# A linear-attention and gated feed-forward kernel: batch 1 turned wholly by DMA, its q loaded first, batch 2's loads queued later

## Chip, cores, metric

One core of a Trainium2 chip. The metric is device microseconds (us) for one execution.

## The reference, cut to what matters

```python
B, H, S, D, KP = 8, 8, 1024, 64, 64           # q, k, v: [B, H, S, D] float32
k_proj = einsum('ks,bhsd->bhkd', E, k);  v_proj = einsum('ks,bhsd->bhkd', F, v)
attn = softmax(q @ k_proj.T / sqrt(D));  a = attn @ v_proj
x = a.transpose(0, 2, 1, 3).reshape(8192, 512)
g = x @ w_gate;  out = (g * sigmoid(g) * (x @ w_val)) @ w_out      # d_ff = 1536
```

## The kernel before

The feed-forward part is 16 tiles of 512 tokens (two per batch). For each of the 12 slices of `d_ff` TensorE does a gate group, a value group (4 matmuls of 128x512 each) and, of the tile before, one group of the output product. After each gate group, and again after each value group with its output group, there is a *slot*, in which pieces of the next batch's attention are put. Batches count from 0, so `b == 1` is the second batch.

q and the normalised scores must each be turned (transposed) before TensorE can use them. Two ways exist: on TensorE (`u_T`, `u_A`, with a copy out of PSUM) or by a DMA transpose from SyncE (`u_TD`, `u_AD`). `BY_DMA` lists the halves that go by DMA.

```python
BY_DMA = [(b, ch) for b in range(1, B) for ch in range(CH)][1:]      # all but (1, 0)

def u_TD(b, ch):                                    # q half by DMA
    t = aw.tile([P, 2 * H, P], BF16, name="qTd", tag="qTd")
    nc.sync.dma_start_transpose(out=t[:], in_=qb[b, ch][:].rearrange("p h j d -> p (h j d)"))
def u_AD(b, ch):                                    # normalised scores by DMA -> AT
    ...
# loads are issued by GpSimd in program order, among its normalisations (u_N)
load_wo(0); load_wo(1); load_k(1)
...
put(20, load_q, 1, 0); put(20, load_v, 1); put(20, load_q, 1, 1)
for b in range(2, B):
    s0 = 48 * (b - 1) - (12 if b == 2 else 24)
    put(s0, load_k, b); put(s0 + 2, load_v, b); put(s0 + 4, load_q, b, 0); put(s0 + 6, load_q, b, 1)
```

`u_KV` projects k and v (8 matmuls each, on `kb` and `vb`), `u_KT` turns the projected k, `u_S` computes scores, `u_R` and `u_N` normalise them, `u_PV` is the product with v (`pv`). SyncE also issues every output store, in one stream with the DMA transposes.

The softmax here doesn't subtract the row's maximum and nothing guards it: scores larger than these inputs give would overflow.

Of the kernel before, what the change touches and what calls it, by code (L numbers as in the profile page):

```python
# [15 lines left out]
B = 8  # L16
# [11 lines left out]
CH = 2  # L28
CW = 512
NIT = B * CH * NFT  # L30
BY_DMA = [(b, ch) for b in range(1, B) for ch in range(CH)][1:]


@with_exitstack
def kernel(
# [49 lines left out]
    def load_k(b, h0=0, h1=H):  # L85
        if h0 == 0:
            kb[b] = kv_pool.tile([P, H, NJ, D], BF16, name="kb", tag="kb")
        nc.gpsimd.dma_start(  # L88
            out=kb[b][:, h0:h1].rearrange("p h j d -> p h (j d)"),
            in_=k[b, h0:h1].rearrange("h (p j) d -> p h (j d)", j=NJ),  # L90
        )
# [10 lines left out]
    def load_q(b, ch, parts=1):  # L102
        t = q_pool.tile([P, H, 4, D], BF16, name="qb", tag="qb")
        qb[b, ch] = t
        n = H // parts
        for i in range(parts):
            nc.gpsimd.dma_start(  # L107
                out=t[:, i * n : (i + 1) * n].rearrange("p h j d -> p h (j d)"),
                in_=q[b, i * n : (i + 1) * n].rearrange("h (p c j) d -> p c h (j d)", c=2, j=4)[:, ch],
            )  # L110

    def load_w_gv(c0, c1, which=(0, 1)):
        cs = slice(c0 * P, c1 * P)
        for wsrc, wdst in [((moe_w_gate, wg), (moe_w_val, wv))[i] for i in which]:
            nc.gpsimd.dma_start(
                out=wdst[:, :, cs],
                in_=wsrc[:, cs].rearrange("(t p) c -> p t c", p=P),
            )

    def load_wo(i):  # L120
        nc.gpsimd.dma_start(
            out=wo[:, 6 * i : 6 * (i + 1), :],
            in_=moe_w_out[6 * i * P : 6 * (i + 1) * P, :].rearrange("(t p) c -> p t c", p=P),
        )
# [93 lines left out]
    def u_S(b, u, at="a"):  # L218
        ch, w = divmod(u, 4)
        g, i = divmod(w, 2)  # L220
        ps = bank(at, [P, 4, P], FP32, "sc")
        if (b, ch) in BY_DMA:
            t = qT[b, ch, "d"][:].rearrange("p (h i) t -> p i h t", i=2)[:, i, 4 * g : 4 * g + 4]
# [163 lines left out]
    def put(s, fn, *a):  # L387
        slots[s].append((fn, a))

    def place(b):  # L390
        s0 = 48 * (b - 1)
        if b == 1:
            put(30, u_TD, 1, 1)
            put(34, u_KV, 1, "k")
            put(36, u_KT, 1)
            put(40, u_KV, 1, "v")
            sa = (37, 38, 39, 40, 48, 50, 52, 54)
            tt = (35, 36, 37, 38)
            ta = (41, 42, 43, 44)
            put(57, u_AD, 1, 1)  # L400
            sp = (43, 44, 45, 46, 66, 67, 68, 69)
        else:
            put(s0, u_KV, b)
            put(s0 + 3, u_KT, b)
            o = 14 if b == 2 else 6
            put(s0 + (3 if b == 2 else -6), u_TD, b, 0)
            put(s0 + (5 if b == 2 else -4), u_TD, b, 1)
            sa = [s0 + o + 3 * j for j in range(NJ)]
            put(sa[3] + 4, u_AD, b, 0)
            put(sa[7] + 4, u_AD, b, 1)  # L410
            sp = [s0 + i for i in (39, 41, 43, 45, 57, 59, 61, 63)]
        for j in range(NJ):
            if (b, j // 4) not in BY_DMA:
                put(tt[j], u_T, b, j)
                put(ta[j], u_A, b, j)
            put(sa[j], u_S, b, j)
            put(sa[j] + 1, u_R, b, j)
            put(sa[j] + 1, u_N, b, j)
        for i in range(8):
            put(sp[i], u_PV, b, i // 4, i % 4)  # L420
# [5 lines left out]
    with tc.manual_schedule():  # L426
        load_k(0, 0, 4)
        ef = []
        for which, src in (("E", E), ("F", F)):
            raw = const.tile([KP, S], FP32, name=f"{which}raw")  # L430
            nc.sync.dma_start(out=raw[:], in_=src)
            ef.append(raw)
        zeros = const.tile([P, CW], BF16, name="zeros")
        nc.vector.memset(zeros[:], 0.0)
        make_identity(nc, ident_fp[:])
        make_identity(nc, ident_bf[:])
        for i in range(2):
            nc.vector.memset(BD[i][:], 0.0)
            nc.vector.memset(BDV[i][:], 0.0)

        def turn(which):
            for half in range(2):
                ps = bank("v", [P, 4, KP], FP32, "efp")
                for i in range(4):
                    j = 4 * half + i
                    nc.tensor.transpose(
                        out=ps[:, i, :],
                        in_=ef[which][:, bass.ds(j, P, step=NJ)],
                        identity=ident_fp[:KP, :KP],
                    )  # L450
                js = slice(4 * half, 4 * half + 4)
                copy((nc.scalar, nc.vector)[which], (ET, FT)[which][:, js, :], ps[:])

        def warm(n):

            ps = bank("v", [P, CW], FP32, "warm")
            for _ in range(n):
                nc.tensor.matmul(
                    out=ps[:], lhsT=zeros[:, 0:P], rhs=zeros[:],
                    start=True, stop=True,  # L460
                )


        load_k(0, 4, 8)
        load_q(0, 0, 2)
        load_v(0, (0, 4, 8))
        load_w_gv(0, 1)
        load_w_gv(1, 2)
        load_w_gv(2, 4)
        warm(8)  # L470
        turn(0)
        turn(1)
        warm(7)
        u_KV(0, "k", (0, 4), at="y")
        warm(2)
        u_KT(0, at="v", prs=(0, 2))
        warm(2)
        u_KV(0, "k", (4, 8), at="y")
        warm(2)
        u_KT(0, at="v", prs=(2, 4))  # L480
        u_T(0, 0, "a", nc.scalar)
        u_T(0, 1, "a", nc.vector)
        u_T(0, 2, "a", nc.scalar)
        u_S(0, 0, "g")
        u_T(0, 3, "v", nc.vector)
        u_S(0, 2, "g")
        u_S(0, 1, "a")
        u_S(0, 3, "a")
        u_R(0, 0)
        u_N(0, 0)  # L490
        u_R(0, 2)
        u_N(0, 2)
        load_w_gv(4, 6, (0,))
        u_KV(0, "v", (0, 4), at="y")
        warm(1)
        u_A(0, 0, nc.scalar)
        u_R(0, 1)
        u_N(0, 1)
        u_R(0, 3)
        u_N(0, 3)  # L500
        u_A(0, 2, nc.scalar)
        u_KV(0, "v", (4, 8), at="y")
        load_w_gv(4, 6, (1,))
        load_q(0, 1)
        load_w_gv(6, 8)
        load_w_gv(8, 10)
        load_w_gv(10, 12)
        load_wo(0)
        load_wo(1)
        load_k(1)  # L510
        warm(1)
        u_PV2(0, 0, 0, 0, nc.scalar)
        u_PV2(0, 0, 1, 0, nc.vector)
        u_A(0, 1, nc.scalar)
        u_A(0, 3, nc.vector)
        f_mm(0, 0, 0, 0)
        f_mm(0, 0, 1, 0)
        u_PV2(0, 0, 0, 1, nc.scalar)
        u_PV2(0, 0, 1, 1, nc.vector)
        f_mm(0, 1, 0, 0)  # L520
        f_mm(0, 1, 1, 0)

        for i, u in enumerate(range(4, 8)):
            put(12 + i, u_T, 0, u)
            put(14 + i, u_S, 0, u)
            put(15 + i, u_R, 0, u)
            put(15 + i, u_N, 0, u)
            put(19 + i, u_A, 0, u, nc.scalar)
        put(21, u_PV, 0, 1, 0)
        put(22, u_PV, 0, 1, 1)  # L530
        put(23, u_PV, 0, 1, 2)
        put(23, u_PV, 0, 1, 3)
        put(20, load_q, 1, 0)
        put(20, load_v, 1)
        put(20, load_q, 1, 1)
        for b in range(1, B):
            place(b)
        for b in range(2, B):
            s0 = 48 * (b - 1) - (12 if b == 2 else 24)
            put(s0, load_k, b)  # L540
            put(s0 + 2, load_v, b)
            put(s0 + 4, load_q, b, 0)
            put(s0 + 6, load_q, b, 1)

        for s in slots:
            slots[s].sort(key=lambda x: x[0] not in (load_k, load_v, load_q))


        ypart = defaultdict(list)
        for c in range(B * CH - 1):  # L550
            for n in range(NFT):
                f = n if c else 4 + (2 * n + 1) // 3
                ypart[(c + 1) * NFT + f].append((c, n))

        for t in range(NIT):
            c, f = divmod(t, NFT)
            i = 1 if t < 2 else None
            f_g(c, f, i)
            run_slot(2 * t)
            f_v(c, f, i)  # L560
            for a in ypart.pop(t, ()):
                f_y(*a)
            run_slot(2 * t + 1)
        for n in range(9):
            f_y(B * CH - 1, n)
        f_y_last(B * CH - 1, 3)
        assert not slots and not ypart
# [29 lines left out]
```

## Time and profile before

| | before |
|---|---|
| time, median (lowest to highest) | 573.88 us (572.83 to 574.1, 3 runs) |
| TensorE busy, granted clock | 561.2 of 572.4 us, 1.000 |
| k, v of batch 2 issued / landed | 47.9, 48.7 / 67.5, 74.1 us |
| projection of batch 2 starts | 88.2 us |

The waits of TensorE in the kernel before (what waited, on what: us in total, times, longest). All lie in the first 22 us; none is a wait in mid-kernel.

```profile
PE kvp L147 <- DMA kb<-in_k_dram: 1.3, 2, 1.0
PE warm L458 <- DVE zeros L434: 1.2, 1, 1.2
PE kvp L147 <- DMA vb<-in_v_dram: 1.0, 2, 0.6
PE qTp L193 <- DMA qb<-in_q_dram: 0.4, 1, 0.4
```

### The profile page before, as it was taken

The page shows a single profiled execution, that of the slowest core. Times are in us where ns is not written, and L with a number is a line of the kernel's source. Part 1 is how long each engine was busy: PE and PEld are TensorE (multiplying, and loading weights), DVE is VectorE, ACT ScalarE, POOL GpSimd, SP SyncE. Part 2 cuts the span into 40 slices and gives each one's busy share as a digit, 9 for nine tenths or more (in the row PEclk, how much of TensorE's full clock was granted, in tenths as well). Part 3 has the DMA queues.
Part 4 walks back from the last instruction along what each step waited for, and adds up shares of the span by engine and source line. Part 5 has one row for each costly group of instructions (what it writes and reads, how often), then busy time and mean ns, then how long its engine had stood idle before and what let it go on. Part 6 is the DMA issues. An engine that isn't in the chain of part 4 may idle for free.

```text
span 572.4 us, 7867 instructions
## 1 busy us (share of the span) xinstructions
PE 561.2 (98%) x2910; PEld 268.6 (47%) x2967; DVE 336.8 (59%) x580; ACT 237.0 (41%) x416; POOL 107.9 (19%) x121
## 2 busy tenths in 40 slices
PE   8899999999999999999999999999999999999997
PEld 4654544444444444444444444444444444444444
DVE  2787566666466744766556665567546674554550
ACT  1655444353425434444335434354342543443232
POOL 6734131234002400124001330023200220000000
PEclk9999999999999999999999999999999999999999
DMA  9999993539901698037951399204990124100012
GB/s 160 196 200 206 201 161 74 93 64 196 201 37 41 110 190 157 18 75 129 187 108 38 59 179 195 63 22 88 197 176 37 42 52 74 38 37 25 31 39 92
DMA packets 105927, 61.34 MB, mean 107 GB/s; under 512 B 58016, under 2 KB 97696, under 8 KB 105888
## 3 DMA queue, kind: packets, MB, share of 16 engines
q0 software_dynamic: 42288, 29.89, 36.1%
q1 hardware_dynamic: 63312, 30.68, 25.1%
q8 instruction: 23, 0.38, 0.3%
q10 hardware_dynamic: 288, 0.26, 0.1%
q14 instruction: 16, 0.13, 0.1%
HBM read 60.29 MB, written 16.78 MB: 135 GB/s over the span
## 4 chain that ended last, share of the span: by engine, by line
PE 94%; DMA 2%; POOL 1%; ACT 1%; issue 1%; DVE 0%; POOLq 0%
PE yps L360 29%; PE vps L322 29%; PE gps L322 29%; PE kvp L147 3%; PE sc L227 2%; DMA vb<-in_v_dram 2%; PE pv L285 2%; PE aTp L274 0%; ACT xT L135 0%; PE qTp L193 0%; POOL kb L88 0%; PE kTp L172 0%; POOL qb L107 0%; ACT th L334 0%; PE pv L300 0%
## 5 line engine op out<-in xcount | busy, mean ns | idle before, releaser
L341 DVE SCALAR_TENSOR_TENSOR s<-th,gps 128x512 f32<-128x512 f32 x192 | 130.5, 680 | 138.0 <-ACT th L334 137.8
L322 PE MATMUL gps<-xT,wg 128*128 128x512 bf16 (+1 forms) x755 | 195.7, 377 | 1.2
L322 PE MATMUL vps<-xT,wv 128*128 128x512 bf16 (+1 forms) x761 | 195.9, 377 | 0.8
L360 PE MATMUL yps<-wo,hT 128*128 128x512 bf16 (+2 forms) x761 | 191.5, 376 | 0.8
L334 ACT ACTIVATE th<-gps 128x512 f32<-128x512 f32 x192 | 114.6, 597 | 162.6 <-PE gps L322 155.1
L346 DVE TENSOR_TENSOR hT<-s,vps 128x512 bf16<-128x512 f32 x192 | 132.0, 688 | 22.1 <-PE vps L322 1.5
L360 PEld LDWEIGHTS <-hT 128*128 128x128 bf16 x780 | 76.2, 98 | 89.9
L258 POOL TENSOR_TENSOR AAd<-ee,rr 128x512 bf16<-128x512 f32 x52 | 54.1, 1040 | 319.5 <-issue 168.4
L322 PEld LDWEIGHTS <-wv 128*128 128x128 bf16 x776 | 73.9, 98 | 82.9 <-issue 3.3
L322 PEld LDWEIGHTS <-wg 128*128 128x128 bf16 x776 | 74.0, 98 | 81.3 <-issue 0.6
L370 ACT ACTIVATE ysb<-yps 128x512 f32<-128x512 f32 (+1 forms) x65 | 38.4, 590 | 78.1 <-PE yps L360 74.4
L135 ACT CAST xT<-pv 128x512 bf16<-128x512 f32 x62 | 36.1, 585 | 51.3 <-PE pv L285 50.3
L242 DVE TENSOR_REDUCE zz<-ee 128x8 f32<-128x512 f32 x64 | 43.5, 679 | 17.9 <-ACT ee L231 17.9
L231 ACT ACTIVATE ee<-sc 128x512 f32<-128x512 f32 x64 | 37.9, 595 | 17.4 <-PE sc L227 17.4
L285 PE MATMUL pv<-AT,BDV 128*128 128x512 bf16 x60 | 22.6, 379 | 0.1
L227 PEld LDWEIGHTS <-qTd 128*128 128x128 bf16 x208 | 16.0, 98 | 12.3
L227 PE MATMUL sc<-BD,qTd 128*128 128x128 bf16 x208 | 20.1, 219 | 0.1
L135 DVE CAST BDV<-kvp 64x256 bf16<-64x256 f32 x14 | 6.0, 426 | 22.1 <-ACT ks L157 19.1
L258 POOL TENSOR_TENSOR AA<-ee,rr 128x512 bf16<-128x512 f32 x10 | 10.3, 1038 | 35.2 <-DVE rr L244 33.6
L147 PE MATMUL kvp<-kb,ET 128*64 128x512 bf16 (+1 forms) x72 | 15.5, 357 | 1.3 <-DMA kb<-in_k_dram 1.3
L244 DVE RECIPROCAL rr<-zz 128x8 f32<-128x8 f32 x64 | 13.0, 203 | 6.2
L147 PE MATMUL kvp<-vb,FT 128*64 128x512 bf16 (+1 forms) x72 | 15.5, 358 | 1.0 <-DMA vb<-in_v_dram 1.0
(49 smaller groups left out, 144.8 us busy)
## 6 DMA issues: line engine op xcount, KB each, us to landing
out_dram<-ysb SPq DMA_DIRECT2D x63, 256.0 KB, 2.3
qb<-in_q_dram POOLq DMA_DIRECT2D x15, 512.0 KB, 16.6
kb<-in_k_dram POOLq DMA_DIRECT2D x7, 1024.0 KB, 11.6
vb<-in_v_dram POOLq DMA_DIRECT2D x7, 1024.0 KB, 14.2
wo<-in_moe_w_out_dram POOLq DMA_DIRECT2D x2, 768.0 KB, 14.8
wg<-in_moe_w_gate_dram POOLq DMA_DIRECT2D x5, 256.0 KB, 10.4
wv<-in_moe_w_val_dram POOLq DMA_DIRECT2D x5, 256.0 KB, 10.4
kb<-in_k_dram POOLq DMA_DIRECT2D x2, 512.0 KB, 8.7
```

What stands on the lines that cost most here:

```text
L135: (nc.scalar.copy if eng is nc.scalar else eng.tensor_copy)(out=out, in_=in_)
L147: nc.tensor.matmul(out=t[lo : lo + 64, h0:h1].rearrange("p h d -> p (h d)"), lhsT=w[:, j, :], rhs=src[b][:, h0:h1, j, :], start=(j == 0), ...
L227: nc.tensor.matmul(out=ps[:, n, :], lhsT=t[:, n, :], rhs=BD[b % 2][:, 4 * g + n, :], start=True, stop=True)
L231: nc.scalar.activation(out=e[:].rearrange("p h j k -> p (h j k)"), in_=ps[:].rearrange("p a k -> p (a k)"), func=AF.Exp, scale=scale,)
L242: nc.vector.reduce_sum(out=z[:], in_=e[:], axis=AX.X)
L258: eng.tensor_tensor(out=a.rearrange("p j h k -> p h j k"), in0=ee.pop((b, u))[:], in1=rr.pop((b, u))[:].unsqueeze(3).to_broadcast([P, 4, 2 ...
L322: nc.tensor.matmul(out=ps[:, ts], lhsT=(wg, wv)[w][:, kt, f * P : (f + 1) * P], rhs=x[:, kt, ts], start=(kt == 0), stop=(kt == NKT - 1),)
L334: nc.scalar.activation(out=th[:], in_=ps[:], func=AF.Tanh, scale=0.5)
L341: nc.vector.scalar_tensor_tensor(out=s1[:], in0=th[:], scalar=1.0, in1=g[:], op0=ALU.add, op1=ALU.mult)
L346: nc.vector.tensor_tensor(out=hT[c][:, f, :], in0=s1[:], in1=ps[:], op=ALU.mult)
L360: nc.tensor.matmul(out=yy[c][:, cs], lhsT=hT[c][:, f, i * P : (i + 1) * P], rhs=wo[:, f, cs], start=(f == 0), stop=(f == NFT - 1),)
L370: nc.scalar.activation(out=ysb[:, cs], in_=yy[c][:, cs], func=AF.Copy, scale=0.5)
```

## The change

Intent: take the last transposes after batch 0 off TensorE, by turning batch 1's first half by DMA as well. To have its q in time, that half is loaded ahead of k and the output weights. To keep batch 1's DMA transposes free of other traffic, batch 2's loads are put at slots 50 to 52, and batch 2's projection, scores and transposes move back.

```diff
-BY_DMA = [(b, ch) for b in range(1, B) for ch in range(CH)][1:]
+BY_DMA = [(b, ch) for b in range(1, B) for ch in range(CH)]
@@ place(b), b == 1 (u_T, u_A of the first half removed)
-            put(34, u_KV, 1, "k"); put(36, u_KT, 1)
+            put(22, u_TD, 1, 0)
+            put(29, u_KV, 1, "k"); put(32, u_KT, 1)
-            sa = (37, 38, 39, 40, 48, 50, 52, 54)
+            sa = (35, 36, 37, 38, 48, 49, 50, 51)
+            put(41, u_AD, 1, 0); put(45, u_TD, 1, 1)
@@ place(b), b >= 2 (only b == 2 changes)
-            put(s0, u_KV, b); put(s0 + 3, u_KT, b)
-            o = 14 if b == 2 else 6                     # scores start at s0 + o
+            put(s0 + (12 if b == 2 else 0), u_KV, b)
+            put(s0 + (15 if b == 2 else 3), u_KT, b)
+            o = 17 if b == 2 else 6
@@ order of loads
+        load_q(1, 0)
+        load_k(1)
         load_wo(0)
         load_wo(1)
-        load_k(1)
-            s0 = 48 * (b - 1) - (12 if b == 2 else 24)
+            s0 = 48 * (b - 1) - 24
+            at = (50, 50, 51, 52) if b == 2 else (s0, s0 + 2, s0 + 4, s0 + 6)
```

(Cut: two q-transpose slots of batch 2, other slots of batch 1.)

More of the change, by code (lines that the diff above doesn't have):

```diff
@@ L392, in place @@
         if b == 1:
-            put(30, u_TD, 1, 1)
-            put(34, u_KV, 1, "k")
-            put(36, u_KT, 1)
+            put(22, u_TD, 1, 0)
+            put(29, u_KV, 1, "k")
+            put(32, u_KT, 1)
             put(40, u_KV, 1, "v")
-            sa = (37, 38, 39, 40, 48, 50, 52, 54)
-            tt = (35, 36, 37, 38)
-            ta = (41, 42, 43, 44)
-            put(57, u_AD, 1, 1)
-            sp = (43, 44, 45, 46, 66, 67, 68, 69)
-        else:
-            put(s0, u_KV, b)
-            put(s0 + 3, u_KT, b)
-            o = 14 if b == 2 else 6
-            put(s0 + (3 if b == 2 else -6), u_TD, b, 0)
-            put(s0 + (5 if b == 2 else -4), u_TD, b, 1)
+            sa = (35, 36, 37, 38, 48, 49, 50, 51)
+            put(41, u_AD, 1, 0)
+            put(45, u_TD, 1, 1)
+            put(56, u_AD, 1, 1)
+            sp = (44, 45, 46, 46, 66, 67, 68, 69)
+        else:
+            put(s0 + (12 if b == 2 else 0), u_KV, b)
+            put(s0 + (15 if b == 2 else 3), u_KT, b)
+            o = 17 if b == 2 else 6
+            put(s0 + (12 if b == 2 else -6), u_TD, b, 0)
+            put(s0 + (14 if b == 2 else -4), u_TD, b, 1)
             sa = [s0 + o + 3 * j for j in range(NJ)]
@@ L412, in place @@
         for j in range(NJ):
-            if (b, j // 4) not in BY_DMA:
-                put(tt[j], u_T, b, j)
-                put(ta[j], u_A, b, j)
             put(sa[j], u_S, b, j)
@@ L532 @@
         put(23, u_PV, 0, 1, 3)
-        put(20, load_q, 1, 0)
         put(20, load_v, 1)
@@ L538 @@
         for b in range(2, B):
-            s0 = 48 * (b - 1) - (12 if b == 2 else 24)
-            put(s0, load_k, b)
-            put(s0 + 2, load_v, b)
-            put(s0 + 4, load_q, b, 0)
-            put(s0 + 6, load_q, b, 1)
+            s0 = 48 * (b - 1) - 24
+            at = (50, 50, 51, 52) if b == 2 else (s0, s0 + 2, s0 + 4, s0 + 6)
+            put(at[0], load_k, b)
+            put(at[1], load_v, b)
+            put(at[2], load_q, b, 0)
+            put(at[3], load_q, b, 1)
         for s in slots:
```

## The prediction

> **What bounds the kernel now.** I read the busy shares first, then the clock and DMA slices, then the order of time on TensorE.
>
> ```profile
> PE 561.2 (98%) x2910; PEld 268.6 (47%) x2967; DVE 336.8 (59%) x580; ACT 237.0 (41%) x416; POOL 107.9 (19%) x121
> PEclk9999999999999999999999999999999999999999
> DMA  9999993539901698037951399204990124100012
> PE 94%; DMA 2%; POOL 1%; ACT 1%; issue 1%; DVE 0%; POOLq 0%
> ```
>
> TensorE is busy 98% of the span at full clock, and the chain that ended last is 94% TensorE. A busy record is not peak use, so I also looked at starts: from 30 us on, one group of four 128x512 matmuls follows another every 0.86 us. The waits of TensorE sum to under 5 us and all lie before 22 us. So time changes in two ways only: TensorE work removed (worth its start-to-start time), or a hole put into TensorE (costs its whole length, since nothing later can catch up). The DMA slices are full from 0 to 86 us, so in that stretch loads are late rather than early.
>
> **The removed work**, from TensorE's timeline:
>
> ```profile
> 63.08 0.39 PE L193 MATMUL qTp<-ident_bf,qb 128*128 128x128 bf16 x4
> 63.30 1.03 PE L322 MATMUL gps<-xT,wg 128*128 128x512 bf16 x3
> 75.77 0.39 PE L274 MATMUL aTp<-ident_bf,AA 128*128 128x128 bf16 x4
> 76.00 1.03 PE L322 MATMUL gps<-xT,wg 128*128 128x512 bf16 x4
> ```
>
> The printed 0.39 includes the pipeline's tail. The next group starts 0.22 us after, so a group of four transposes costs 0.22 us of TensorE.
>
> **What sets the DMA times**, from SyncE's timeline, GpSimd's timeline, and the times to landing:
>
> ```profile
> 62.12 7.33 SPq L205 DMA_TRANSPOSE qTd<-qb  x1
> qTd<-qb SPq DMA_TRANSPOSE x1, 13.0
> 88.23 1.71 SPq L205 DMA_TRANSPOSE qTd<-qb  x1
> qTd<-qb SPq DMA_TRANSPOSE x1, 4.4
> 122.18 0.94 POOL L88 DMA_DIRECT2D kb<-in_k_dram  x1
> 126.34 8.32 SPq L212 DMA_TRANSPOSE AT<-AAd  x1
> AT<-AAd SPq DMA_TRANSPOSE x1, 17.2
> 144.65 0.38 PE L285 MATMUL pv<-AT,BDV 128*128 128x512 bf16 x1
> kb<-in_k_dram POOLq DMA_DIRECT2D x7, 1024.0 KB, 11.6
> vb<-in_v_dram POOLq DMA_DIRECT2D x7, 1024.0 KB, 14.2
> ```
>
> A transpose lands in 4.3 to 5.3 us alone, and in 13.0 to 17.2 us with k, v and q loads in flight. The tightest place today is batch 2: its attention transpose lands at 126.34 + 17.2 = 143.5 us and the product that needs it starts at 144.65, one microsecond later.
>
> **What the skill says.** "DMA: Bandwidth & Descriptors", section "Issuing engines are not separate DMA queues": transfers issued by SyncE and GpSimd run on the same 16 engines and interleave. The trace agrees (4.4 against 13.0 us above). The same page, "Anatomy of one DMA", fits a GpSimd load as 2.0 us plus bytes over 436 GB/s, 6.8 us for the 2.1 MB read of one k. The trace has 11.6 us, so I use that. "TensorE: Matmul & The Clock Gate", section "HAM oscillation": an idle gap of more than about 3.4 us can drop TensorE to half clock until it has been busy as long again. The trace shows a slow start only (the first eight 128x512 warm-up matmuls take 3.59 us, against 0.216 us from start to start later); it has no such gap in mid-kernel. The same page's "PE-mode transpose" gives about 275 ns for a 128x128 transpose in a kernel's context; here four issue in 220 ns.
>
> **The change part by part.** Batches count from 0: the change turns all of batch 1 by DMA and delays the loads of batch 2. A slot is the place in TensorE's order after one group of four gate or value matmuls; slot 24 begins the second of the 16 feed-forward tiles. Needs and landings are in us from the span's start.
>
> 1. Removed: four groups of q transposes and four of attention transposes, 8 x 0.22 = 1.76 us of TensorE. All of it counts. The copies that go with them on ScalarE and VectorE count for nothing (41% and 59% busy).
>
> 2. Earlier loads, the first q half ahead of k and the output weights. Landings in the kernel before, from each issue plus its time: output weights 42.9 and 46.7, k 51.7. So 0.75 MB of bf16 takes 3.8 us and 1 MB takes 5.0 when the queue is full, and 0.5 MB takes 2.6. The last gate weights land near 39. New order: q half 41.7, k about 47.6, output weights about 52 and 56 (0.5 to 1 us added for the q transpose beside them). Needs: the k projection moves five slots forward, to 53.4 us; the output weights are first used at 58.9 and 61.5; the q transpose starts at 41.7, lands by 55, and is needed at 63.3. All hold by 4 us or more: nothing gained, nothing lost.
>
> 3. First attention half of batch 1 by DMA. I count TensorE forward from 51.63 us (gate group 14, unmoved) with 0.864 us per group, 1.85 per projection, 0.22 per score. The fourth score ends at 68.0. In the trace a normalised score ends 4.4 to 5.7 us after its score matmul, so the transpose starts about 72.6, with no loads in flight, and lands at 77 to 78. The product that needs it is at 79.2. The second q transpose waits for an output store at about 79.6 and lands at 84 to 85; needed at 86.1. Both hold, by 1 to 2 us.
>
> 4. **Loads of batch 2.** GpSimd's stream in the changed kernel has them after the fifth normalised score (slot 49). Before, k and v were issued at 47.9 and 48.7 us. Now: fifth score ends at 86.35, plus 4.5 gives k issued at about 90.8, v at 91.7. From that score to the projection of k and v (moved back 12 slots) TensorE has two groups, three scores, five full rounds of 2.59 us and one group: 16.2 us, so it wants both at 102.6, 11.8 us after k's issue. In the trace k alone needs 11.6 us, and v behind it 1 MB more (5.0), less the time the queue fills better, plus an output store and part of an attention transpose: 15.5 to 17 us. v lands near 107.3. **Hole of about 4.7 us** (3.5 to 6).
>
> 5. After it: q of batch 2 lands about 110, its transpose starts then behind the second attention transpose and lands at 114 to 117; its first score wants it at 116.6 (shifted by the hole). Perhaps 0.5 us lost.
>
> 6. **Attention transpose of batch 2** moves to slot 78, which on SyncE stands behind the output store of slot 77. Before, it was issued 4.2 us after k of batch 3 and landed 21.3 us after it. In batches 3 to 6 it is issued 9.1 us after the next batch's k and lands at 24.4 to 26.0. Now it would be issued about 10.5 us after, so I take 25.2. The product that wants it comes 22.5 us after k in the kernel before; one score more lies between now, 22.7. **Hole of about 2.5 us.**
>
> 7. Clock: hole 4 is longer than the skill's 3.4 us window, so a half-clock stretch may follow. I put 0.7 us on it.
>
> Sum: -1.76 + 4.7 + 0.5 + 2.5 + 0.7 = +6.6 us, so 580.5; I say 580.0, since the first hole has more room to be shorter than longer.
>
> **Rivals.**
>
> - *Everything is hidden.* Only the 1.76 us count: 572.1 us. For it: the changed order leaves the transposes of batch 1 free of loads, the point of the move. Against it: v would have to land within 11.8 us of k's issue, and no pair in the trace does.
> - *The late hole does not come.* If the attention transpose of batch 2 keeps its 13 us or gets more bandwidth as the loads run out, the second hole vanishes: 577.5 us.
> - *More goes wrong.* The q half delays the output weights past 58.9 us, or a transpose of batch 1 takes 13 us in place of 5 because an output store lies beside it, or the clock stays low for several windows: 584 to 588 us. The 5.3 us of a transpose beside a store in the trace speaks against the second.
>
> **Range and chances.** The saving is certain to 0.2 us. First hole 3.5 to 6, second 0 to 3.5, the small ones 0 to 3: 575.5 to 584.5. Faster by 2% would need 11.5 us and only 1.76 are removed: 0.01. Slower by 2% needs 585.4, that is 13.2 us of holes where I count 8.4: 0.08. Within 2%: 0.91.
>
> **What would show it.** Right: TensorE busy time falls by about 2 us, the 32 transposes are gone, k and v of batch 2 are issued near 91 us, the waits of TensorE list v (line L147) with 4 to 5 us near 102 us, and a product of attention and v (L285) waits 2 to 3 us for a DMA near 147 us. Wrong in step 4: no wait at the second projection, or v landing before 103 us. Wrong in step 3: a wait of L285 or L227 on a transpose between 63 and 90 us. Wrong in step 2: a wait of the output matmuls (L360) on their weights near 59 us. Wrong in step 7: matmuls after the hole at 0.22 us from the first one on means no clock loss.

## More of the kernel before

GpSimd in the kernel before (start, duration of the issue). These two loads of batch 2 are issued 40 us ahead of their use: nothing in GpSimd's stream held them, so they ran ahead of the slots 36 and 38 in which they stand.

```profile
47.88 0.90 POOL L88 DMA_DIRECT2D kb<-in_k_dram  x1
48.74 0.91 POOL L97 DMA_DIRECT2D vb<-in_v_dram  x1
```

## The result, and the profile after

| | before | after |
|---|---|---|
| time, median (lowest to highest) | 573.77 us (572.83 to 574.1, 4 runs) | 582.45 us (580.67 to 583.32, 4 runs) |
| profiled span, granted clock | 572.4 us, 1.000 | 581.6 us, 0.991 |
| k, v of batch 2 issued / v landed | 47.9, 48.7 / 74.1 us | 89.6, 90.5 / 106.6 us |

The ratio is 1.015, 95% interval 1.0119 to 1.0181: slower by 1.5%, inside the 2% band. (A ratio is the mean time of one kernel's fast runs over that of the other's of the same rounds, so it is not quite the ratio of the medians.)

The changed kernel's busy shares, clock, DMA load and chain (the chain of work that ended last, followed back from the last instruction):

```profile
PE 569.1 (98%) x2935; PEld 268.1 (46%) x2935; DVE 335.2 (58%) x576; ACT 235.1 (40%) x412; POOL 107.9 (19%) x121
PEclk9999999799899999999999999999999999999999
DMA  9999568949760399107980379413991033010002
PE 91%; DMA 5%; ACT 1%; DVE 1%; issue 0%; POOL 0%; DVEq 0%; ACTq 0%; POOLq 0%
```

TensorE has less work but more busy time: that is the clock row's 7 and 8, in the slices from 102 to 116 us and from 145 to 160 us. (The size of the rise, 569.1 against 561.2 us, is not to be used: the trace before lacks some records, 2910 matmuls beside 2967 weight loads.) DMA went from 2% to 5% of the chain. Its waits name the places; these two are new:

```profile
PE kvp L147 <- DMA vb<-in_v_dram: 4.5, 1, 4.5
PE pv L285 <- DMA AT<-AAd: 2.3, 1, 2.3
```

The first one on GpSimd's timeline, with v's time to landing, and on TensorE's timeline:

```profile
88.56 1.04 POOL L258 TENSOR_TENSOR AAd<-ee,rr 128x512 bf16<-128x512 f32 x1 [17.20 <-DVE rr L244]
89.55 0.94 POOL L88 DMA_DIRECT2D kb<-in_k_dram  x1
90.48 0.88 POOL L97 DMA_DIRECT2D vb<-in_v_dram  x1
vb<-in_v_dram POOLq DMA_DIRECT2D x1, 1024.0 KB, 16.1
```

```profile
101.74 0.40 PE L147 MATMUL kvp<-kb,ET 128*64 128x512 bf16 x1
106.63 0.58 PE L147 MATMUL kvp<-vb,FT 128*64 128x512 bf16 x1 [4.49 <-DMA vb<-in_v_dram]
106.64 0.63 PE L147 MATMUL kvp<-kb,ET 128*64 128x512 bf16 x1
107.01 0.63 PE L147 MATMUL kvp<-vb,FT 128*64 128x512 bf16 x1
...
110.13 1.89 PE L322 MATMUL vps<-xT,wv 128*128 128x512 bf16 x4
111.81 1.25 PE L360 MATMUL yps<-wo,hT 128*128 128x512 bf16 x4
112.91 1.03 PE L322 MATMUL gps<-xT,wg 128*128 128x512 bf16 x4
```

In the kernel before, k's and v's first matmuls start together:

```profile
88.21 0.40 PE L147 MATMUL kvp<-kb,ET 128*64 128x512 bf16 x1
88.21 0.40 PE L147 MATMUL kvp<-vb,FT 128*64 128x512 bf16 x1
```

GpSimd sat idle for 17.20 us waiting for the fifth score of batch 1, and the loads stand behind it. They were issued as soon as that score was normalised, and v landed at 90.48 + 16.1 = 106.6 us; TensorE wanted it at 101.74. After the wait the k-v pairs come 0.43 us apart in place of 0.22, and the next value group takes 1.68 us to the next start in place of 0.86.

The second, on SyncE's and TensorE's timelines:

```profile
136.96 6.40 SPq L212 DMA_TRANSPOSE AT<-AAd  x1
AT<-AAd SPq DMA_TRANSPOSE x1, 15.0
148.69 1.03 PE L360 MATMUL yps<-wo,hT 128*128 128x512 bf16 x4
151.99 0.39 PE L285 MATMUL pv<-AT,BDV 128*128 128x512 bf16 x1 [2.28 <-DMA AT<-AAd]
152.22 1.03 PE L322 MATMUL gps<-xT,wg 128*128 128x512 bf16 x4
153.08 1.77 PE L322 MATMUL vps<-xT,wv 128*128 128x512 bf16 x4
154.65 1.91 PE L360 MATMUL yps<-wo,hT 128*128 128x512 bf16 x4
```

136.96 + 15.0 = 151.96, and the product starts at 151.99. Again slow groups follow, 1.57 and 1.70 us from start to start, but only after one gate group at full rate (0.86 us).

The account, from start to start in the two profiles (the start-up before the first full gate group, at 26.88 and 25.99 us, is left out, as it differs from run to run):

| stretch | after minus before |
|---|---|
| first full gate group to fifth score of batch 1 (26.88 to 87.89 us; 25.99 to 85.21) | -1.79 |
| the wait for v, start to start (106.63 - 101.74, in place of 0) | +4.89 |
| slow matmuls after it (1.68 in the projection, where v's first matmul to the next group took 3.50 us, and 1.82 at full rate in experiment 3; 0.81 and 0.24 in the next two groups) | +2.73 |
| the wait for the attention transpose (151.99 - 148.69 - 0.86) | +2.44 |
| slow matmuls after it (0.71 + 0.84 + 0.14) | +1.69 |
| sum; the spans less the start-up differ by (581.6 - 25.99) - (572.4 - 26.88) | +9.96; +10.09 |

### The profile page after: what moved, and what is told of

Read it like the earlier page. It is cut to its first block, busy times and chain, and to the rows that moved or that the text cites. A ratio compares the mean times of both kernels' runs of the same rounds, so it can differ in the third digit from the quotient of the medians.

```text
span 581.6 us, 7859 instructions
## 1 busy us (share of the span) xinstructions
PE 569.1 (98%) x2935; PEld 268.1 (46%) x2935; DVE 335.2 (58%) x576; ACT 235.1 (40%) x412; POOL 107.9 (19%) x121
## 4 chain that ended last, share of the span: by engine, by line
PE 91%; DMA 5%; ACT 1%; DVE 1%; issue 0%; POOL 0%; DVEq 0%; ACTq 0%; POOLq 0%
PE yps L360 27%; PE vps L322 27%; PE gps L322 27%; PE kvp L147 3%; DMA vb<-in_v_dram 3%; DMA AT<-AAd 3%; PE pv L285 2%; PE sc L227 2%; PE warm L455 1%; ACT xT L135 0%; PE kTp L172 0%; DVE zz L242 0%; ACT th L334 0%; PE efp L443 0%; PE aTp L274 0%
## 5 line engine op out<-in xcount | busy, mean ns | idle before, releaser
L322 PE MATMUL vps<-xT,wv 128*128 128x512 bf16 (+1 forms) x776 | 199.1, 379 | 0.0
L322 PE MATMUL gps<-xT,wg 128*128 128x512 bf16 (+1 forms) x776 | 198.0, 377 | 0.2
L360 PE MATMUL yps<-wo,hT 128*128 128x512 bf16 (+1 forms) x780 | 195.6, 377 | 0.0
L258 POOL TENSOR_TENSOR AAd<-ee,rr 128x512 bf16<-128x512 f32 x56 | 58.2, 1041 | 355.4 <-issue 166.1
L227 PEld LDWEIGHTS <-qTd 128*128 128x128 bf16 x224 | 17.2, 98 | 13.2
L227 PE MATMUL sc<-BD,qTd 128*128 128x128 bf16 x224 | 21.6, 219 | 0.0
L147 PE MATMUL kvp<-vb,FT 128*64 128x512 bf16 (+1 forms) x72 | 17.2, 385 | 4.5 <-DMA vb<-in_v_dram 4.5
L147 PE MATMUL kvp<-kb,ET 128*64 128x512 bf16 (+1 forms) x72 | 17.2, 383 | 0.0
L107 POOL DMA_DIRECT2D qb<-in_q_dram x17 | 15.1, 892 | 0.6 <-DMA wv<-in_moe_w_val_dram 0.6
```

What stands on the lines that cost most here:

```text
L147: nc.tensor.matmul(out=t[lo : lo + 64, h0:h1].rearrange("p h d -> p (h d)"), lhsT=w[:, j, :], rhs=src[b][:, h0:h1, j, :], start=(j == 0), ...
L227: nc.tensor.matmul(out=ps[:, n, :], lhsT=t[:, n, :], rhs=BD[b % 2][:, 4 * g + n, :], start=True, stop=True)
L258: eng.tensor_tensor(out=a.rearrange("p j h k -> p h j k"), in0=ee.pop((b, u))[:], in1=rr.pop((b, u))[:].unsqueeze(3).to_broadcast([P, 4, 2 ...
L322: nc.tensor.matmul(out=ps[:, ts], lhsT=(wg, wv)[w][:, kt, f * P : (f + 1) * P], rhs=x[:, kt, ts], start=(kt == 0), stop=(kt == NKT - 1),)
L360: nc.tensor.matmul(out=yy[c][:, cs], lhsT=hT[c][:, f, i * P : (i + 1) * P], rhs=wo[:, f, cs], start=(f == 0), stop=(f == NFT - 1),)
```

## The experiments

The theory: two waits made by batch 2's delay, and the clock lost after them, are the whole loss. The rivals: the waits come from the added DMA transposes colliding with loads; the slow matmuls have another cause; the early q costs something. The first four runs shared chip and rounds (kernel before 574.06 us, 7 runs), the last four likewise (573.32 us, 11 runs). The changed kernel was not run again beside them, so comparisons with its time go across rounds.

### 1. k and v of batch 2 early

```diff
-            at = (50, 50, 51, 52) if b == 2 else (...)
+            at = (34, 34, 51, 52) if b == 2 else (...)
```

> Only edit to the changed kernel: k and v of batch 2 are queued at slot 34 (ahead of the normalised scores of batch 1) in place of slot 50. Theory (the first hole is the late issue of these two loads): k and v are issued near 46 us and land by 76 us, the 4.5 us wait of L147 for v near 102 us is gone, the projection runs at 0.22 us a pair from its start, and the time falls by 4.5 us of hole and up to 2.7 us of half clock: 575 to 578 us. The second hole (L285 on the attention transpose of batch 2, 2.3 us) stays. The attention transpose of batch 1's first half now meets the tail of v and may land up to 2 us late for its product. Rival (the loads were delayed for good reason: the transposes of batch 1 collide with them): a new wait of 5 us or more at L285 near 78 us or L227 near 85 us, and the time stays at 581 us or more.

Measured: 575.54 us (574.07 to 577.16), ratio to before 1.0031 (1.0000 to 1.0063). The wait for v at the projection of batch 2 is gone (0.9 us of waits for v remain, at the start-up), 0.6 us appears at the first product of batch 1, and the second hole is there. The rival that the delay was needed falls. One part went unlike the expectation: the four runs fall in two pairs, 574.07 and 574.09 (granted clock 1.000 both) against 576.99 and 577.16 (0.997 and 0.994). The profiled run is one of the first pair; its TensorE timeline around the second hole:

```profile
144.41 0.39 PE L285 MATMUL pv<-AT,BDV 128*128 128x512 bf16 x1 [2.39 <-DMA AT<-AAd]
144.63 1.03 PE L322 MATMUL gps<-xT,wg 128*128 128x512 bf16 x4
145.50 1.03 PE L322 MATMUL vps<-xT,wv 128*128 128x512 bf16 x4
146.36 1.03 PE L360 MATMUL yps<-wo,hT 128*128 128x512 bf16 x4
```

The same hole as in the changed kernel, 2.4 us, here with no slow group after it (0.86 us from start to start). So a hole of this length sometimes costs clock and sometimes not. Where the other pair of runs lost its 3 us is not shown. Their lower mean clock does not place it: a slow start-up lowers the mean too (experiment 4's profile has 0.996 with its one low slice at the very start). And the profiled run has the shortest start-up of all, 25.07 us, so up to 1.8 us of the 3 may lie there.

### 2. Products of batch 2 later

```diff
+            if b == 2:
+                sp[:4] = [s0 + i for i in (42, 43, 44, 45)]
```

> Only edit to the changed kernel: the first four attention products of batch 2 stand at slots 90, 91, 92, 93 in place of 87, 89, 91, 93, some 3.9 us later for the first of them. Theory (the second hole is the attention transpose landing about 2.3 us after its first product wants it): the 2.3 us wait is gone, with up to 1.7 us of half clock after it, and the time falls by 2.3 to 4 us to 578.5 to 580 us. The first hole stays at 4 to 5 us. Rival (TensorE is held at this place by something else, such as the buffer of the product, or the wait only moves): a wait of 1 us or more at the moved product, time within 0.5 us of 582.4.

Measured: 578.31 us (577.4 to 579.86), ratio 1.0074 (1.0052 to 1.0096). The wait on the attention transpose is gone; the wait for v is still 4.4 us. The time lies 4.1 us below the changed kernel's median, just past the upper end of the expected gain. TensorE was held there by nothing but the transpose.

### 3. The holes filled with matmuls of zeros

```diff
+    FILL = {60: 16, 87: 7}      # matmuls of zeros into a spare bank
     def run_slot(s):
+        fill(FILL.get(s, 0))
```

> Only edit to the changed kernel: 16 matmuls of zeros (3.5 us) stand just ahead of the projection of batch 2 and 7 (1.5 us) just ahead of the first attention product of batch 2, where TensorE would wait 4.5 and 2.3 us for a DMA. Theory (the idle holes drop the TensorE clock, and this costs up to 4.4 us beyond the holes): the waits shrink to about 1.0 and 0.8 us, the arrival of v and of the transpose stay at about 106.6 and 152 us less what the clock had cost, the pairs of the projection run at 0.22 us in place of 0.43 us, and the time falls by 2 to 4.4 us to 578 to 580.5 us. Rival (the slow matmuls after the holes have another cause, for example DMA writes beside them, or the idle time does not matter): they stay slow and the time stays at 582 us or rises.

Measured: 581.24 us (580.35 to 582.1), ratio 1.013 (1.011 to 1.015). The work is useless on purpose; the result stays correct. TensorE's timeline:

```profile
102.54 3.62 PE L425 MATMUL fill<-zeros 128*128 128x512 bf16 x16
106.09 0.40 PE L147 MATMUL kvp<-kb,ET 128*64 128x512 bf16 x1
107.18 0.38 PE L147 MATMUL kvp<-vb,FT 128*64 128x512 bf16 x1 [0.69 <-DMA vb<-in_v_dram]
...
109.00 1.04 PE L322 MATMUL vps<-xT,wv 128*128 128x512 bf16 x4
109.87 1.03 PE L360 MATMUL yps<-wo,hT 128*128 128x512 bf16 x4
...
118.41 0.40 PE L227 MATMUL sc<-BD,qTd 128*128 128x128 bf16 x4 [2.00 <-DMA qTd<-qb]
```

v comes at about the same time (107.2 us against 106.6), and the projection and the groups after it run at full rate. So idleness made the slow matmuls after the first hole; what landed beside them did not. The three profiles with that hole unfilled (4.4 to 4.7 us idle: the changed kernel, experiments 2 and 8) all have them. After the second hole the groups run at full rate as well, but that shows nothing, as experiments 1 and 8 do so with this hole unfilled. The time fell by about 1 us only, below the 2 to 4.4 us expected, and its interval overlaps that of the changed kernel. Between the two profiles 0.9 us of gain is covered by start-up: from the first full gate group to the end this run takes 580.3 - 26.89 = 553.4 us, the changed kernel 555.6, 2.2 us less. The last line says why it is not more: the first score of batch 2 now waits 2.00 us for its transposed q, which is issued only when q has landed behind k and v. In the changed kernel this wait was not there because TensorE arrived later, on its slow clock. Of the first 2.73 us of slow matmuls, then, 2.0 us only stood in the place of another wait.

### 4. The load order alone

```diff
 (kernel before)
+        load_q(1, 0)
+        load_k(1)
         load_wo(0)
         load_wo(1)
-        load_k(1)
...
-        put(20, load_q, 1, 0)
```

> Edit to the kernel before: only the load order of the change, the first q half of batch 1 and k of batch 1 ahead of the output weights; nothing else. Theory (the early order costs nothing and gains nothing, as every transfer has microseconds to spare): 573.2 to 574.3 us, no wait of the output matmuls on their weights near 57 to 61 us. Rival (the output weights come too late without the room that the moved projections make): the output weights land near 55 us or later, and L360 waits 1 us or more at 56.8 or 61.4 us, time 575 us or more.

Measured: 573.26 us (572.59 to 573.65), ratio 0.999 (0.9972 to 1.0007); no wait on the output weights. This part of the change costs nothing.

### 5. Experiments 1 and 2 together

> Both edits together on the changed kernel: k and v of batch 2 queued at slot 34, and the first four attention products of batch 2 at slots 90 to 93. Theory (the two holes and the half clock after them are the whole of what the change lost): neither long wait is left, only the 0.6 us at the first attention product of batch 1 where the tail of v meets its transpose; the clock stays at 1.0; the time is that of the kernel before less the 1.76 us of transposes plus 0.6: 572 to 573.5 us. Rival (a further loss was hidden behind the two holes, as the 2.0 us wait on the q transpose was in the run with filled holes): a new wait of 1 us or more, and 574 us or more.

Measured: 572.45 us (571.61 to 573.77), ratio to before 0.9985 (0.9972 to 0.9998). Its busy shares and clock:

```profile
PE 562.7 (99%) x2935; PEld 266.6 (47%) x2935; DVE 335.0 (59%) x576; ACT 235.1 (41%) x412; POOL 107.9 (19%) x121
PEclk9999999999999999999999999999999999999999
```

No wait on a DMA is left past the start-up, not even the 0.6 us at batch 1's first product, and the clock is 1.000 in all runs. From the first full gate group to the end it takes 570.6 - 26.70 = 543.9 us against 545.5 before, 1.6 us less: the 1.76 us of transposes. This version beats both kernels, the one before by 0.15%, at the edge of what the runs can tell.

### 6. k early, v late

```diff
-            at = (34, 34, 51, 52) if b == 2 else (...)      (experiment 5)
+            at = (34, 50, 51, 52) if b == 2 else (...)
```

> As the run with both edits, but only k of batch 2 is queued at slot 34; v stays at slot 50, behind the normalised scores. Theory: k lands near 70 us, before the attention transpose of batch 1 starts at 71.4 us, so the 0.6 us wait at its first product is gone; v, alone ahead of q, is issued near 90 us and lands 9 to 11.6 us later, against a need near 102 us, so it waits 0 to 1 us; 571.5 to 573 us. Rival (v needs as long as with k ahead of it, 16 us): a wait of 3 us or more at L147 near 102 us and 575 us or more.

Measured: 574.7 us (573.75 to 576.2), ratio 1.002 (1.0006 to 1.0034). v behaves as expected (10.7 us to landing, no wait for it at the projection of batch 2). The time does not: v still stands ahead of q, and the first score of batch 2 waits for q's transpose.

```profile
114.19 0.40 PE L227 MATMUL sc<-BD,qTd 128*128 128x128 bf16 x4 [2.56 <-DMA qTd<-qb]
```

I had left q out of the expectation; it is the wait that experiment 3 had just uncovered.

### 7. Batch 2 in its old place

```diff
 (changed kernel; b == 2 only)
-            put(s0 + 12, u_KV, b); put(s0 + 15, u_KT, b); o = 17; u_TD at s0 + 12 and s0 + 14
+            put(s0, u_KV, b); put(s0 + 3, u_KT, b); o = 14; u_TD at s0 + 8 and s0 + 10
-            at = (50, 50, 51, 52)
+            at = (34, 34, 50, 51)
```

> Batch 1 as in the changed kernel, batch 2 placed as in the kernel before (projection at slot 48, scores from slot 62, products from 87), with k and v of batch 2 queued at slot 34 and its q at slots 50 and 51. Theory (the turns of batch 1 by DMA cost nothing themselves, only the delay of batch 2 did): no wait of TensorE above 1 us after 30 us, 572 to 573.5 us. Rival (batch 2 had to be delayed, because in its old place its transposes collide with those of batch 1): a wait of 2 us or more at L227 or L285 between 78 and 150 us and 575 us or more.

Measured: 575.28 us (574.36 to 577.47), ratio 1.0036 (1.0021 to 1.0052). The expectation fails: there is one wait of 2.7 us, at the first score of batch 2, for its transposed q. SyncE issued the attention transpose of batch 1's second half at 98.40 us and q's transposes behind it, at 104.29 us; in experiment 5 they go at 102.95 us and the scores stand three slots later. The first half of q had landed by 98.9 us (93.13 + 5.8), so its transpose did not wait for the load: it stood behind the attention transpose in SyncE's stream, whose issue took 5.79 us beside the load of q's second half (1.77 us for the same transpose in the kernel before, at 103.24 us). In this order on SyncE there was no room for batch 2 in its old place. Another order, or earlier q loads, was not tried.

### 8. The delay of batch 2 alone

```diff
 (kernel before; b == 2 only, batch 1 untouched)
+ the changed kernel's slots of projection, scores and q transposes, and its loads at (50, 50, 51, 52)
```

> Kernel before with only the delays of batch 2 taken from the change: its loads at slots 50 to 52, its projection at 60, its scores from 65; batch 1's first half is still turned by TensorE. Theory (the delays alone make the holes): k issued near 92 us, a wait for v at L147 of 4 to 5 us near 104 us, a wait on the attention transpose of 2 to 3 us, part of the clock lost after them; 582 to 584.5 us, about the time of the changed kernel plus the 1.76 us that it saves. Rival (the holes need the added DMA transposes beside the loads): waits under 1 us and 574 to 576 us.

Measured: 583.34 us (581.8 to 583.67), ratio 1.0166 (1.0152 to 1.0179). Its TensorE timeline has both holes at the size of the changed kernel:

```profile
108.39 0.58 PE L147 MATMUL kvp<-vb,FT 128*64 128x512 bf16 x1 [4.70 <-DMA vb<-in_v_dram]
152.27 0.39 PE L285 MATMUL pv<-AT,BDV 128*128 128x512 bf16 x1 [2.18 <-DMA AT<-AAd]
```

The holes need none of batch 1's added transposes. The delay alone makes them.

## Why the prediction was right, and where a size was off

- **Step 1, the removed work: right.** -1.76 us said, -1.79 us in the profile up to the fifth score, -1.6 us in experiment 5 over the whole run. Its sign, TensorE's busy time falling by about 2 us, did not come: the slow matmuls raised it, and missing records had lowered the figure before.
- **Step 2, the load order: right.** Nothing gained or lost (experiment 4). One landing was later than said: batch 1's first q transpose took 18.0 us, not 13, and landed at 59.1 us; it was needed at 62.5.
- **Step 3, batch 1's transposes: right.** In the changed kernel they landed in 4.3 and 5.7 us and no product or score waited for them.
- **Step 4, the first hole: right.** 4.7 us said, 4.89 us from start to start; k issued at 89.6 (90.8 said), v wanted at 101.7 (102.6), landed at 106.6 (107.3). All three came about 1 us early, so the difference held. Experiments 1 and 8 show that its cause is the late issue.
- **Step 6, the second hole: right.** 2.5 us said, 2.44 us found. The path was as told: the transpose landed 25.1 us after k of batch 3 was issued at 126.86 us (25.2 said). Experiment 2 removes the hole.
- **Step 7, the clock: mechanism right, size wrong.** 0.7 us was put on it; the profiled run has 2.73 + 1.69 = 4.4 us of slow matmuls. I had counted only the longer hole, and only a chance of it. The short hole, too, was followed by a slow stretch in the changed kernel, though not in experiments 1 and 8. (That TensorE must be busy as long again is told in the page's section "What's actually happening", not in "HAM oscillation". Here the slow stretches after the long hole were about 5.5, 5.6 and 2.7 us, an estimate from the 2.73, 2.8 and 1.3 us lost at half rate in the changed kernel and experiments 2 and 8.)
- **Step 5, q's transpose: 0.5 us said, none seen.** It was there, and larger (2.0 us in experiment 3), but the slow clock hid it. This is why undoing the clock loss gained so little. Steps 5 and 7 were both sized too small, but their losses fell on the same time and counted once; that was luck.
- **The sum.** 580.0 said, 582.45 measured, inside the range. In the profiled run (583.3 us) the clock term was 3.7 us too small; less the 0.5 us of step 5, that is 3.2 of its 3.3 us above the forecast. The runs at clock 0.991 took 583.3 us, those at 0.997 took 580.7 and 581.6; where these two lost less was not profiled.

The rival "everything is hidden" was wrong as told: v did not land in time. The transposes of batch 1 did become free of loads, as the change intended, but experiment 1 shows that they need not have been quite so free: with k and v ahead of them they cost 0.6 us in one profile and nothing in another.

## What to carry to other kernels

On an engine that is busy 98% of the time a removed instruction gives back its start-to-start time and no more, while one load issued too late costs its whole wait: before moving a load back, count the work between its new issue and its use, and compare it with the time that the same load took, behind the same neighbours, in the trace. A load's place is decided by what stands ahead of it in its issuer's stream, not by the slot it is written in. And a hole can hide another one behind it, so check a repair for the wait that it uncovers.

## What the Trainium skill lacked or had wrong

- "TensorE: Matmul & The Clock Gate", section "HAM oscillation", gives the rule as no idle gaps of more than about 3.4 us. Here a gap of 2.28 us was followed by about half rate, one group later, in the changed kernel (groups of 1.57 and 1.70 us in place of 0.86), and gaps of 2.00 to 2.73 us were not in five other profiles (experiments 1, 3, 6, 7 and 8). After each of the three gaps of 4.43 to 4.70 us half rate came at once.
- "DMA: Bandwidth & Descriptors", section "Anatomy of one DMA": an estimate from its fit is 6.8 us for 2.1 MB read and 4.4 us for 1.05 MB. Loads that read float32 and write bf16 took 10.7 us for the first size with two more loads behind it (experiment 6), and 6.5 us for the second (q of batch 2 in experiment 5). The pair of k and v, 4.2 MB, was in after 17.0 us, where the fit gives 11.6. Other transfers ran beside each of these, so the fit for a lone load is not shown wrong; I found no figure in the page for several such loads at once.
- No page that I found tells how a DMA transpose fares beside a load: 0.5 MB took 4.3 us alone and 15.0 to 18.0 us beside k, v, q or weight loads in the changed kernel.
